# Sliding-window attention and a multiplicative FFN on one core: loads issued in one run, fold transposes a step ahead of their products, o units on column halves of TensorE in batches 0 and 1, and a new order of work for batch 1

**Chip, cores, metric.** One core of a Trainium2 chip. The metric is device time in microseconds (us) from launch to end. The "span" of a profile is 1.5 to 2 us shorter: first to last instruction.

## The reference, cut to what matters

```python
def _attn_ref(q, k, v):                    # (8, 8, 576, 64) each
    scores = (1 / sqrt(64)) * q @ k^T      # masked to 0 <= row - col < 64
    return softmax(scores) @ v

def _moe_ref(x, w1, w2, w3, w_out):        # x: (4608, 512), the attention's output
    return ((x @ w1) * (x @ w2)) @ w3 @ w_out      # d_ff = 1024
```

The kernel folds `w3 @ w_out` into one matrix `wc` once, runs attention batch by batch, and feeds nine groups of 512 tokens to the FFN. The part up to the end of token group 0 (batches 0 and 1, the fold, first FFN group) is written out by hand; I call it the prologue. After it comes a loop in which attention units lie between FFN steps.

Some names: a unit is one call of `scores` or `values` (four heads, 192 queries); units 0 to 5 are batch 0, 6 to 11 batch 1, and the first two of a batch have 768 columns, the others 1024. An FFN step is one call of `ffn_ab` or `ffn_o` (8 matmuls of 512 columns). A filler is a matmul of `keep_busy`, whose result nobody uses. A bank is the piece of PSUM that a matmul writes; the next writer waits until it is read (1.34 us at one unit of the run no_s). 1/sum is taken as Exp(-Ln(sum)).

## The kernel before: the parts that matter

```python
def load_rows(b, which):                         # q, k or v of a batch, cast to fp16 by the DMA
    t = sb.tile([P, 2, TI * D], FP16, name="rows")          # two buffers
    for hh in range(2):
        nc.gpsimd.dma_start(out=t[:, hh], in_=big_rows(which, b, hh))
    ...
def values(d, pool=None):                        # "o unit": probabilities x v, then 1/sum
    ...
    for jj in range(2):
        first = True
        for a in range(2):                       # v16 holds [v0 | ones | v1 | ones]
            c0 = 0
            for bi, (k0, q0, n, _) in enumerate(seg):
                o0 = a * 192 + q0 - q_base
                nc.tensor.matmul(o_ps[:, jj, o0:o0 + n],
                                 v16[:, si * 2 + bi, j0 + jj, a * D:a * D + P],   # 128 columns: o and sum
                                 pt[:, a, jj, c0:c0 + n],
                                 start=first, stop=(bi == 1), skip_group_check=True)
                first = False
                c0 += n
    ...
    nc.scalar.activation(y[0:D], o_ps[D:P, :, 0:192], AF.Ln)
    nc.scalar.activation(y[D:P], o_ps[0:D, :, 192:384], AF.Ln)
    nc.scalar.activation(r, y, AF.Exp, scale=-1.0)
    nc.vector.tensor_tensor(xs[0:D], o_ps[0:D, :, 0:192], r[0:D], ALU.mult)
    nc.vector.tensor_tensor(xs[D:P], o_ps[D:P, :, 192:384], r[D:P], ALU.mult)

def fold_t(fc, cp=dve_cp):      # 8 transposes of w3 into PSUM, copied back over w3
def fold_mm(fc, half, cp, nf=1):# 8 products of 256 columns (x nf), copied to wc

# fold stage (cut)
fold_t(0); scores(2); load_rows(1, "k"); fold_mm(0, 0, dve_cp)
fold_t(1); scores(3); fold_mm(1, 0, dve_cp)
fold_t(2); scores(4); fold_mm(2, 0, act_cp)
...
for d in range(3, 6):
    fold_mm(2 * d - 6, 1, dve_cp, 2)
    values(d, ps_s if d % 2 else None)
fold_mm(6, 1, dve_cp, 2)
for hh in range(2):
    cast_qk(1, "k", hh, dve_cp)
load_rows(1, "v")
for i in range(2):
    load_w12(i, 1)               # second halves of w1 and w2
# batch 1 (cut)
ffn_ab(0, 0)
transposes(1, "k", 0, 1, 2, ...)
ffn_ab(0, 1)
for hh in range(2):
    cast_qk(1, "q", hh, dve_cp)
transposes(1, "q", 0, 1, 2, ...)
ffn_ab(0, 2); scores(6); cast v; transposes v; ffn_ab(0, 3); scores(7) ...
```

## Time and profile before

| | us |
|---|---|
| device time, median of 3 runs (later, with more runs: 310.1 to 311.4) | 310.06 |
| first fold transposes start | 16.2 |
| eighth first-half fold product ends | 42.2 |
| second FFN step ends | 56.2 |
| first o unit of batch 1 starts | 72.2 |
| second token group starts | 95.6 |

These are start times on TensorE in the timeline; an end is the last start plus its length by starts (for the second FFN step, its end in the profile). From the last row on TensorE is busy nearly without a break (20.00 of the 20 us from 120 to 140), so what matters is how soon it comes. The lines behind it stand in the prediction.

### The profile page before, as it was taken

The numbers are of one execution on the slowest core, as the hardware profiler recorded it, in microseconds if no ns is written. First come the engines' busy times: TensorE is split into PE (matmuls) and PEld (weight loads), VectorE is DVE, ScalarE is ACT, GpSimd is POOL, SyncE is SP. The second block draws the span as 40 slices with busy tenths as digits, with TensorE's granted clock in tenths as the row PEclk, the third lists the DMA queues.
The fourth block names the chain that finished last, engine by engine and source line by source line (L and its number), as shares of the span: only waits on it lengthen the run. The fifth ranks groups of instructions, "written<-read, shape, count | busy, mean of one in ns | idle before, by whom it ended". The sixth has DMA issues, their size and how long they took to land.

```text
span 308.2 us, 6193 instructions
## 1 busy us (share of the span) xinstructions
PE 282.2 (92%) x2386; PEld 165.9 (54%) x2386; DVE 193.1 (63%) x300; ACT 173.1 (56%) x286; POOL 176.1 (57%) x212
## 2 busy tenths in 40 slices
PE   7675889778898999999999999999999999999992
PEld 7564786435464555555555588655555544454441
DVE  1534568735488676678878776667876765555531
ACT  2545544147843764777667756558657766642310
POOL 9799100267971995669687946486867544320400
PEclk9999799879999999999999999999999999999999
DMA  6999900999416993829483954092049003003012
GB/s 242 224 210 203 205 4 4 174 336 219 26 70 203 317 83 81 291 85 73 146 305 28 121 193 186 34 170 15 3 84 133 1 5 135 0 2 138 1 38 106
DMA packets 43906, 37.69 MB, mean 122 GB/s; under 512 B 29488, under 2 KB 33584, under 8 KB 43872
## 3 DMA queue, kind: packets, MB, share of 16 engines
q0 software_dynamic: 34560, 11.14, 32.8%
q1 hardware_dynamic: 9312, 26.10, 23.5%
q8 instruction: 20, 0.33, 0.4%
q14 instruction: 14, 0.11, 0.1%
HBM read 38.80 MB, written 9.44 MB: 156 GB/s over the span
## 4 chain that ended last, share of the span: by engine, by line
PE 76%; DVE 9%; ACT 5%; DMA 4%; issue 2%; POOL 2%; POOLq 0%; ACTq 0%; DVEq 0%
PE f_ps L413 36%; PE f_ps L426 20%; PE o_ps L329 5%; PE tp L261 5%; PE s_ps L295 4%; PE f_ps L477 3%; DMA ab<-in_moe_w_dram 3%; POOL v L512 2%; DVE xT L345 2%; DVE kT L265 2%; DMA stage<-in_k_dram 1%; ACT ln_s L339 1%; ACT r L341 1%; DVE xT L344 1%; ACT pt L299 1%
## 5 line engine op out<-in xcount | busy, mean ns | idle before, releaser
L413 PE MATMUL f_ps<-xT,w_sb 128*128 128x512 f16 (+1 forms) x640 | 137.1, 363 | 0.6 <-DVE xT L345 0.6
L307 POOL TENSOR_SCALAR_AFFINE_SELECT pt<-pt 128x512 f16<-128x512 f16 (+1 forms) x64 | 52.3, 818 | 70.6 <-ACT pt L299 70.6
L413 PEld LDWEIGHTS <-w_sb 128*128 128x128 f16 x640 | 60.6, 99 | 53.0 <-issue 4.5
L426 PE MATMUL f_ps<-wc_sb,ab 128*128 128x512 f16 x288 | 66.9, 379 | 0.1
L419 DVE TENSOR_TENSOR ab<-f_ps,a_sb 128x512 f16<-128x512 f32 x72 | 49.8, 692 | 21.2 <-PE f_ps L413 18.3
L299 ACT ACTIVATE pt<-s_ps 128x1024 f16<-128x1024 f32 (+1 forms) x48 | 45.6, 951 | 23.7 <-PE s_ps L295 22.2
L418 ACT COPY a_sb<-f_ps 128x512 f32<-128x512 f32 x72 | 41.7, 579 | 29.3 <-PE f_ps L413 28.7
L309 POOL TENSOR_SCALAR_AFFINE_SELECT pt<-pt 128x512 f16<-128x512 f16 (+1 forms) x64 | 51.9, 811 | 4.4
L344 DVE TENSOR_TENSOR xT<-o_ps,r 64x384 f16<-64x384 f32 x43 | 23.6, 550 | 47.3 <-ACT r L341 47.3
L426 PEld LDWEIGHTS <-ab 128*128 128x128 f16 x288 | 26.8, 98 | 28.2 <-issue 0.3
L338 ACT ACTIVATE ln_s<-o_ps 64x384 f32<-64x384 f32 x43 | 20.9, 487 | 36.8 <-PE o_ps L329 36.1
L428 DVE COPY t2k<-f_ps 128x512 f32<-128x512 f32 x36 | 24.8, 690 | 11.1 <-PE f_ps L426 10.6
L329 PEld LDWEIGHTS <-v 128*128 128x128 f16 x384 | 24.0, 99 | 12.2 <-ACT pt L299 3.9
L329 PE MATMUL o_ps<-pt,v 128*128 128x128 f16 x344 | 24.9, 216 | 1.7 <-DVE xT L345 1.7
L341 ACT ACTIVATE r<-ln_s 128x384 f32<-128x384 f32 x48 | 25.1, 522 | 1.5
L240 POOL DMA_DIRECT2D v<-in_v_dram x30 | 25.4, 854 | 0.0
L345 DVE TENSOR_TENSOR xT<-o_ps,r 64x384 f16<-64x384 f32 x43 | 24.1, 561 | 0.6
L339 ACT ACTIVATE ln_s<-o_ps 64x384 f32<-64x384 f32 x43 | 20.7, 482 | 0.5
L295 PEld LDWEIGHTS <-kT 64*128 64x128 f16 x384 | 10.6, 94 | 16.6 <-issue 15.0
L295 PE MATMUL s_ps<-qT,kT 64*128 64x128 f16 (+1 forms) x384 | 18.2, 214 | 0.5 <-ACT pt L299 0.4
L265 DVE COPY kT<-tp 128x768 f16<-128x768 f16 x17 | 16.2, 951 | 0.0
L225 POOL CAST k<-stage 128x1152 f16<-128x1152 f32 x12 | 13.8, 1151 | 2.0 <-PE tp L261 2.0
(83 smaller groups left out, 230.9 us busy)
## 6 DMA issues: line engine op xcount, KB each, us to landing
out_dram<-t2k SPq DMA_DIRECT2D x36, 256.0 KB
stage<-in_k_dram SPq DMA_DIRECT2D x14, 576.0 KB
stage<-in_q_dram SPq DMA_DIRECT2D x14, 576.0 KB
v<-in_v_dram POOLq DMA_DIRECT2D x24, 128.0 KB, 4.1
w_sb<-in_moe_w_dram POOLq DMA_DIRECT2D x4, 512.0 KB, 13.3
rows<-in_v_dram POOLq DMA_DIRECT2D x4, 288.0 KB, 8.0
ab<-in_moe_w_out_dram POOLq DMA_DIRECT2D x2, 512.0 KB, 11.9
ab<-in_moe_w_dram POOLq DMA_DIRECT2D x2, 512.0 KB, 9.3
```

The source lines that it names most:

```text
L295: nc.tensor.matmul(s_ps[:, a, jj, c0:c0 + n], kT[half, j, k0:k0 + P], qT[half, j, q0:q0 + n], start=True, stop=True, skip_group_check=True)
L299: nc.scalar.activation(pt[:, :, :, 0:w], s_ps[:, :, :, 0:w], AF.Exp, bias=-SHIFT, scale=scale)
L307: nc.gpsimd.affine_select(out=sl, in_=sl, pattern=pat, compare_op=ALU.is_ge, fill=0.0, base=off, channel_multiplier=-1)
L309: nc.gpsimd.affine_select(out=sl, in_=sl, pattern=[[-s, m] for s, m in pat], compare_op=ALU.is_ge, fill=0.0, base=63 - off, channel_multip ...
L329: nc.tensor.matmul(o_ps[:, jj, o0:o0 + n], v16[:, si * 2 + bi, j0 + jj, a * D:a * D + P], pt[:, a, jj, c0:c0 + n], start=first, stop=(bi = ...
L341: nc.scalar.activation(r, y, AF.Exp, scale=-1.0)
L344: nc.vector.tensor_tensor(xs[0:D], o_ps[0:D, :, 0:192], r[0:D], ALU.mult)
L345: nc.vector.tensor_tensor(xs[D:P], o_ps[D:P, :, 192:384], r[D:P], ALU.mult)
L413: nc.tensor.matmul(d[:, f * n + c0:f * n + c1], w[:, dc, (fc + f) * P:(fc + f + 1) * P], xT[:, dc, xc:xc + c1 - c0], start=first, stop=(dc ...
L418: act_cp(a_sb[:, 0:nf * n], a_ps[:, 0:nf * n])
L419: nc.vector.tensor_tensor(ab[:, fc:fc + nf, lo:hi], b_ps[:, 0:nf * n].rearrange("p (f n) -> p f n", f=nf), a_sb[:, 0:nf * n].rearrange("p ...
L426: nc.tensor.matmul(o_ps, ab[:, fc, t * P:t * P + P], wc_sb[:, fc, :], start=(fc == 0), stop=(fc == 7))
```

## The change

Its intent: issue the loads of batch 1 and the second halves of w1 and w2 early and in one run (three row buffers; three output buffers in place of four make room); turn each w3 block a step ahead of its product; shorten the chain after an o unit (Ln, Exp, multiply, up to the FFN's input xT); deal out the work of batch 1 so that TensorE has FFN steps to do while others cast and copy.

```diff
-        t = sb.tile([P, 2, TI * D], FP16, name="rows")
+        t = sb.tile([P, 2, TI * D], FP16, name="rows", bufs=3)
@@ values: for b < SHORT (= 2)
+            for jj in range(2):
+                c0 = 0
+                for bi, (k0, q0, n, _) in enumerate(seg):
+                    o0 = jj * 192 + q0 - q_base
+                    for e in range(2):            # e = 0: o, e = 1: sum
+                        for a in range(2):        # head a goes to column half a
+                            nc.tensor.matmul(o_ps[a * D:a * D + D, e, o0:o0 + n],
+                                             v16[:, si * 2 + bi, j0 + jj, (2 * a + e) * D:(2 * a + e) * D + D],
+                                             pt[:, a, jj, c0:c0 + n], ...)
+                    c0 += n
+            nc.scalar.activation(y, total, AF.Ln)
+            nc.scalar.activation(r, y, AF.Exp, scale=-1.0)
+            nc.vector.tensor_tensor(xs, o, r, ALU.mult)
+            return
@@ fold stage
     scores(2)
-    load_rows(1, "k")
+    fold_t(1, act_cp)
     fold_mm(0, 0, dve_cp)
-    fold_t(1)
     scores(3)
-    fold_mm(1, 0, dve_cp)
+    load_rows(1, "k")
     fold_t(2)
+    fold_mm(1, 0, act_cp)
 ...
     scores(5)
+    load_rows(1, "q")
+    for i in range(2):
+        load_w12(i, 1)
+    load_rows(1, "v")
+    fold_mm(3, 0, act_cp)
+    keep_busy(12)
 ...
-    for d in range(3, 6):
-        fold_mm(2 * d - 6, 1, dve_cp, 2)
+    for d in range(2, 6):
         values(d, ps_s if d % 2 else None)
-    fold_mm(6, 1, dve_cp, 2)
-    for hh in range(2):
-        cast_qk(1, "k", hh, dve_cp)
-    load_rows(1, "v")
-    for i in range(2):
-        load_w12(i, 1)
+        fold_mm(2 * d - 4, 1, dve_cp, 2)
+        if d == 4:
+            for hh in range(2):
+                cast_qk(1, "k", hh, dve_cp)
@@ batch 1: k transposes ahead of the first FFN step; q cast between steps 0 and 1; steps 4 and 5
@@ move ahead of the o units; the k transposes of batch 2 move in between them
```

More of the change, by code (lines that the diff above doesn't have):

```diff
@@ L169 @@
     ND = 6 * B
+    SHORT = 2
     keep = ctx.enter_context(tc.tile_pool(name="keep", bufs=1))
@@ L322, in values @@
             ps_s.tile([P, 2, 512], FP32, name="s_ps")
+        if jp == 0:
+            lns[b, si] = sb.tile([P, NJ, 192], FP32, name="ln_s", bufs=4)
+        y = lns[b, si][:, j0:j0 + 2]
+        r = sb.tile([P, 2, 192], FP32, name="r")
+        x0 = (b * S + q_base) % RING
+        xs = xT[:, j0:j0 + 2, x0:x0 + 192]
+        if b < SHORT:
+            for jj in range(2):
[6 more added lines that the diff above has]
+                                             v16[:, si * 2 + bi, j0 + jj, (2 * a + e) * D:(2 * a + e) * D + D],
+                                             pt[:, a, jj, c0:c0 + n],
+                                             start=(jj == 0 and bi == 0), stop=(bi == 1), skip_group_check=True)
+                    c0 += n
+            o, total = (o_ps[:, e, 0:384].rearrange("p (j n) -> p j n", j=2) for e in range(2))
+            nc.scalar.activation(y, total, AF.Ln)
+            nc.scalar.activation(r, y, AF.Exp, scale=-1.0)
+            nc.vector.tensor_tensor(xs, o, r, ALU.mult)
+            return
         for jj in range(2):
@@ L334, in values @@
                     c0 += n
-        if jp == 0:
-            lns[b, si] = sb.tile([P, NJ, 192], FP32, name="ln_s", bufs=4)
-        y = lns[b, si][:, j0:j0 + 2]
         nc.scalar.activation(y[0:D], o_ps[D:P, :, 0:192], AF.Ln)
         nc.scalar.activation(y[D:P], o_ps[0:D, :, 192:384], AF.Ln)
-        r = sb.tile([P, 2, 192], FP32, name="r")
         nc.scalar.activation(r, y, AF.Exp, scale=-1.0)
-        x0 = (b * S + q_base) % RING
-        xs = xT[:, j0:j0 + 2, x0:x0 + 192]
         nc.vector.tensor_tensor(xs[0:D], o_ps[0:D, :, 0:192], r[0:D], ALU.mult)
@@ L426, in ffn_o @@
             nc.tensor.matmul(o_ps, ab[:, fc, t * P:t * P + P], wc_sb[:, fc, :], start=(fc == 0), stop=(fc == 7))
-        o_sb = sb.tile([P, DM], FP32, name="t2k", bufs=4)
+        o_sb = sb.tile([P, DM], FP32, name="t2k", bufs=3)
         dve_cp(o_sb, o_ps)
@@ L549 @@
     scores(2)
+    fold_t(1, act_cp)
+    fold_mm(0, 0, dve_cp)
+    scores(3)
     load_rows(1, "k")
-    fold_mm(0, 0, dve_cp)
-    fold_t(1)
-    scores(3)
-    fold_mm(1, 0, dve_cp)
     fold_t(2)
+    fold_mm(1, 0, act_cp)
     scores(4)
+    fold_t(3)
     fold_mm(2, 0, act_cp)
-    fold_t(3)
     scores(5)
-    fold_mm(3, 0, dve_cp)
+    load_rows(1, "q")
[4 more added lines that the diff above has]
+    keep_busy(12)
     cast_qk(0, "v", 0, dve_cp)
-    cast_qk(0, "v", 1, act_cp)
-    load_rows(1, "q")
+    cast_qk(0, "v", 1, dve_cp)
     transposes(0, "v", 0, 1, 2, into=spare(ps_v, "o_ps") + [tp_bank()], cps=[dve_cp, act_cp, dve_cp])
     fold_t(4, act_cp)
-    fold_mm(4, 0, dve_cp)
-    keys_of_v(0, [0, 1, 2, 3], spare(ps_v, "o_ps") + spare(ps_s, "s_ps"), [dve_cp, act_cp, dve_cp, act_cp])
     fold_t(5)
+    keys_of_v(0, [0, 1], spare(ps_v, "o_ps"), [act_cp, dve_cp])
+    fold_mm(4, 0, act_cp)
+    keys_of_v(0, [2, 3], spare(ps_s, "s_ps"), [act_cp, dve_cp])
+    fold_t(6)
+    fold_mm(5, 0, dve_cp)
+    fold_t(7, act_cp)
     values(0)
-    fold_mm(5, 0, dve_cp)
-    fold_t(6)
+    fold_mm(6, 0, dve_cp)
     values(1, ps_s)
-    fold_mm(6, 0, dve_cp)
-    fold_t(7)
-    values(2)
     fold_mm(7, 0, dve_cp)
-    for d in range(3, 6):
-        fold_mm(2 * d - 6, 1, dve_cp, 2)
+    for d in range(2, 6):
         values(d, ps_s if d % 2 else None)
-    fold_mm(6, 1, dve_cp, 2)
-    for hh in range(2):
-        cast_qk(1, "k", hh, dve_cp)
-    load_rows(1, "v")
-    for i in range(2):
-        load_w12(i, 1)
+        fold_mm(2 * d - 4, 1, dve_cp, 2)
+        if d == 4:
+            for hh in range(2):
+                cast_qk(1, "k", hh, dve_cp)
     for n in range(3):
         keep_sums(n)
+    transposes(1, "k", 0, 1, 2, into=spare(ps_s, "s_ps") + [tp_bank()])
     ffn_ab(0, 0)
-    transposes(1, "k", 0, 1, 2, into=spare(ps_s, "s_ps") + [tp_bank()])
-    ffn_ab(0, 1)
     for hh in range(2):
         cast_qk(1, "q", hh, dve_cp)
-    load_qk(2, "k", nc.gpsimd.memset)
-    load_qk(2, "q")
+    ffn_ab(0, 1)
     transposes(1, "q", 0, 1, 2, into=spare(ps_v, "o_ps") + [tp_bank()])
@@ L600 @@
     cast_qk(1, "v", 0, dve_cp)
-    cast_qk(1, "v", 1, act_cp)
-    load_v(2, 0, 2, 3)
-    transposes(1, "v", 0, 1, 2, into=spare(ps_v, "o_ps") + [tp_bank()], cps=[dve_cp, act_cp, dve_cp])
+    cast_qk(1, "v", 1, dve_cp)
     ffn_ab(0, 3)
     scores(7)
+    load_qk(2, "k", nc.gpsimd.memset)
+    load_qk(2, "q")
+    transposes(1, "v", 0, 1, 2, into=spare(ps_v, "o_ps") + [tp_bank()], cps=[dve_cp, act_cp, dve_cp])
+    ffn_ab(0, 4)
+    scores(8)
+    load_v(2, 0, 2, 3)
     keys_of_v(1, [0, 1, 2], spare(ps_v, "o_ps") + [tp_bank()], [dve_cp, act_cp, dve_cp])
-    scores(8)
-    keys_of_v(1, [3], [tp_bank()], [dve_cp])
-    steps = [lambda fc=fc: ffn_ab(0, fc) for fc in range(4, 8)] + [lambda t=t: ffn_o(0, t) for t in range(4)]
+    ffn_ab(0, 5)
+    keys_of_v(1, [3], [tp_bank()], [act_cp])
+    steps = [lambda fc=fc: ffn_ab(0, fc) for fc in range(6, 8)] + [lambda t=t: ffn_o(0, t) for t in range(4)]
     for d in range(6, 12):
@@ L620 @@
             cast_qk(2, "kq"[(d - 6) // 2], d % 2, pool_cp)
-    transposes(2, "k", 0, 1, into=spare(ps_v, "o_ps"))
+        if d == 9:
+            transposes(2, "k", 0)
+        if d == 10:
+            transposes(2, "k", 1)
     transposes(2, "k", 2)
@@ L624 @@
         cast_qk(3, "k", hh, pool_cp)
-    steps.pop(0)()
-    store()
-    transposes(2, "q", 0, 1, into=spare(ps_s, "s_ps"))
-    transposes(2, "q", 2)
+    transposes(2, "q", 0, 1, 2, into=spare(ps_v, "o_ps") + spare(ps_s, "s_ps")[0:1])
     load_qk(3, "q")
-    steps.pop(0)()
-    store()
     copy_v(2, 1)
```

## The prediction

> **What bounds the kernel now.** I read the page's busy line first, then the same engines in stretches of 20 us, then the table of waits, then the timeline of the first 110 us. The page shows TensorE as the busiest engine, with 8% of the span free:
>
> ```profile
> span 308.2 us, 6193 instructions
> PE 282.2 (92%) x2386; PEld 165.9 (54%) x2386; DVE 193.1 (63%) x300; ACT 173.1 (56%) x286; POOL 176.1 (57%) x212
> ```
>
> The stretches (time, then busy us of PE, weight loads, DVE, ACT, POOL, then granted clock, DMA share, GB/s) show where the free part lies:
>
> ```profile
> 0.00:20.00 20.00, 14.83 (x218) 13.03 (x219) 7.26 (x10) 8.47 (x10) 16.68 (x26) 1.00 0.97 227
> 20.00:40.00 20.00, 13.78 (x164) 12.00 (x163) 10.08 (x17) 10.23 (x15) 11.70 (x13) 0.91 1.11 192
> 40.00:60.00 20.00, 16.87 (x166) 13.09 (x165) 15.15 (x26) 7.14 (x14) 2.67 (x5) 0.97 0.28 45
> 60.00:80.00 20.00, 15.84 (x142) 8.64 (x142) 9.65 (x16) 12.95 (x20) 13.21 (x18) 0.86 1.09 240
> 80.00:100.00 20.00, 18.66 (x152) 10.14 (x150) 15.33 (x25) 10.60 (x19) 11.58 (x12) 1.00 0.41 109
> 120.00:140.00 20.00, 20.00 (x171) 10.55 (x170) 14.46 (x23) 13.87 (x24) 12.48 (x17) 1.00 0.46 160
> ```
>
> From 100 us on TensorE has no idle time worth naming at full clock: whatever starts that part sooner ends the kernel sooner by as much. All idle time and both dips of the clock (0.91, 0.86) lie in the prologue: folding w3 with w_out, attention of batches 0 and 1, the first 512 tokens of the FFN. The first FFN product of the second token group starts at 95.6 us; 212 us follow. The change touches only that prologue. The table of waits and the timeline name its gaps:
>
> ```profile
> POOL rows L216 <- DVE k L225: 21.6, 1, 21.6
> DVE xT L344 <- ACT r L341: 50.4, 47, 1.7
> PE f_ps L477 <- DVE xT L469: 2.3, 3, 1.8
> PE f_ps L477 <- ACT xT L469: 2.0, 1, 2.0
> ```
>
> ```profile
> 17.59 1.05 PE L477 MATMUL f_ps<-ab 128*128 128x256 f16 x8 [0.46 <-DVE ab L469]
> 53.53 1.07 POOL L216 DMA_DIRECT2D rows<-in_v_dram  x2 [21.55 <-DVE k L225]
> 58.26 0.93 PE L261 MATMUL o_ps<-ident,q 128*128 128x128 f16 x12 [2.05 <-DVE q L225]
> 59.61 3.22 PE L413 MATMUL f_ps<-xT,w_sb 128*128 128x512 f16 x8
> 65.12 0.95 PE L261 MATMUL o_ps<-ident,k 128*128 128x128 f16 x12 [2.01 <-ACT k L225]
> ```
>
> The v load of batch 1 waited 21.6 us for one of two row buffers, and the second halves of w1 and w2 are queued behind it; the DMA was nearly idle meanwhile (45 GB/s in 40 to 60). Each fold product waits for the copy of its own transposes (0.46 to 2.0 us). TensorE then waits twice for 2 us on casts of q and v, after which an 8-matmul block takes 3.2 us in place of 1.9.
>
> [...] after gaps of 2 us with little work around them the same block ran at 3.22 against 1.90 us. [...] The trace has no column tiles; its row halves do pair up: eight 128-column score matmuls take 0.23 us of weight-load time where eight full ones take 0.45. [...]
>
> ```profile
> L338 ACT ACTIVATE ln_s<-o_ps 64x384 f32<-64x384 f32 x43 | 20.9, 487 | 36.8 <-PE o_ps L329 36.1
> L341 ACT ACTIVATE r<-ln_s 128x384 f32<-128x384 f32 x48 | 25.1, 522 | 1.5
> L344 DVE TENSOR_TENSOR xT<-o_ps,r 64x384 f16<-64x384 f32 x43 | 23.6, 550 | 47.3 <-ACT r L341 47.3
> ```
>
> **The change part by part.** I count TensorE work by starts: 0.46 us for a fold transpose, 0.87 for a fold product of one half (1.74 for two), 1.73 for an FFN step, 1.0 for 18 transposes, 0.3 for scores; copies by their rows: fold copy 0.69 on DVE or 1.02 on ACT, a transpose copy 0.95, a cast pair 0.83.
>
> *Short o units, 12 of them.* ACT loses one Ln (0.49), DVE one multiply (0.56): the chain from o to xT falls from 2 x 0.49 + 0.52 + 2 x 0.56 = 2.6 to 1.6 us. TensorE gets 16 half-width pairs for 8 full ones. If halves overlap it stays at 0.45 us; [...] I take 0.85, as the author keeps the old form where TensorE is the bound: +0.4 x 12 = 4.8 us of TensorE work.
>
> *Stage A, first fold transpose (16.2, set by a DMA) to the end of the eighth first-half fold product.* Before: ends at 42.2, with the three units 0 to 2. After: transposes run one step ahead, so a product waits for a copy that is mostly done. Stepping through, with the single score bank freed by ACT's exp (1.02) and ACT now also copying: fold 3 ends at 23.2 (25.3 before), 12 fillers to 23.9, v transposes at 23.9 (26.7), vT copied at 26.7, keys-of-v copies end 30.8, unit 0 at 31.1, unit 1 and products 6 and 7 end at 34.5. Unit 2 is not yet in: gain 7.7.
>
> *Stage B, to the end of the second FFN step.* Four units and four double products at 0.85 + 1.74, 1.0 of k transposes, two steps of 1.73: 34.5 + 10.4 + 1.0 + 3.5 = 49.4, against 56.2. Cumulative gain 6.8.
>
> *Stage C, to the first o unit of batch 1.* Before: 56.2 to 72.2, of which some 5 us are waits on casts, copies and small bank waits and 3 us the half clock; only two FFN steps inside. After: the rows came by about 47 us (1.6 MB more behind a queue that ends at 38.5 us, at the 205 GB/s of that part), casts lie beside FFN steps, four steps fill in: q transposes, 4 x 1.73, three scores, v transposes, 24 key transposes, small waits = 11.9, so 61.3. Two more steps (3.5) are already done: 16.0 + 3.5 - 11.9 = 7.6 gained. Cumulative 14.4.
>
> *Stage D, to the second token group.* Before: 72.2 to 95.6 = 23.4, less those two steps 19.9. After: six units, three scores, two FFN steps and four o steps, 36 transposes: 18.6 us, with POOL as a near tie. POOL has masks of six score units (2 x 2.1 + 4 x 2.25), v loads (4.3) and k casts (2.3) in a row: 54.1 + 20.5 = 74.6 before the last unit may start; TensorE by my count reaches it at 75.9. Gain 1.3; the second group starts at 79.9, 15.7 earlier.
>
> *Other edits.* Three buffers for output rows in place of four: copies are at least 1.7 us apart even at the tail, so I give this nothing. DMA, total bytes: unchanged.
>
> From 15.7 I take off 2.6 for handovers and shared-bank waits that such stepping misses (of the kind that show as 0.2 to 0.6 us all over the timeline). 310.1 - 13.1 = **297.0 us**.
>
> **The rivals.**
> (1) *POOL becomes the bound of stages C and D.* Its work from the first scores of batch 1 on is 20 us that nothing shortens, and batch 2's loads now start only after the second masks, so its first cast might wait. For it: POOL runs from 73 to 88 us without a break now. Against: k of batch 2 has some 9 us to land. If it holds, stage D loses 3 to 5 us: 300 to 302.
> (2) *Column halves are dear.* If halves do not overlap at all[...]: 12 x 0.3 to 0.5 more, 300 to 303.
> (3) *Full gain.* Halves overlap (0.45 a unit) and nothing is missed: 4 to 5 us better than my sum before the deduction, 291 to 292.
> (4) *The idle time is only moved.* The second group begins early, but q of batch 2 or the cast of batch 3 is late, and TensorE waits at 80 to 95 us. Now only about 2 us are lost there; I see no reason for over 3 more.
>
> **Range and chances.** Rivals 1 and 2 together make about 303, rival 3 makes 291: range 291 to 303. Faster by 2% needs under 303.9, that is, 6.2 of the counted 15.7 us: 0.89. Within 2%: 0.09. Slower: 0.02; nothing is added to the TensorE-bound part.
>
> **What would show it.** The second group's first FFN product at 79 to 85 us, and the same 212 us after it; clock near 1.00 from 20 us on and DMA busy to about 47 us without the pause; no POOL wait for a row buffer; fold products waiting under 0.4 us; one Ln and one multiply of 128x384 at about 0.50 and 0.57 us a unit; 16 half-width matmuls in about 0.85 us. I am wrong if the second group starts after 89 us, if a unit holds TensorE over 1.2 us, if the part after it grows by over 3 us, or if POOL or a late load becomes the longest wait in 50 to 80 us.

## The result

293.60 us median (four runs, 292.96 to 295.06) against 310.59 (four runs, 309.82 to 311.32). The ratio is 0.946, 95% interval 0.9413 to 0.9507. Ratios here are the mean time of one kernel's fast runs over that of the other's of the same rounds, so not quite the ratio of the medians quoted. Taken as 5.4% of 310.6, the gain is 16.8 us; I had predicted 13.1.

The page and the stretches of the changed kernel (same columns as before):

```profile
span 293.3 us, 6375 instructions
PE 281.0 (96%) x2494; PEld 165.4 (56%) x2494; DVE 185.3 (63%) x284; ACT 168.4 (57%) x278; POOL 176.5 (60%) x212
```

```profile
20.00:40.00 20.00, 18.94 (x275) 15.86 (x274) 11.65 (x18) 13.18 (x21) 15.66 (x20) 1.00 1.20 207
40.00:60.00 20.00, 19.59 (x208) 12.68 (x206) 16.01 (x25) 8.85 (x15) 4.42 (x9) 1.00 0.40 70
60.00:80.00 20.00, 19.15 (x217) 10.64 (x215) 11.05 (x18) 11.93 (x21) 17.75 (x18) 1.00 1.38 248
80.00:100.00 20.00, 19.31 (x168) 10.17 (x166) 15.68 (x24) 13.34 (x23) 17.52 (x22) 1.00 0.89 215
```

TensorE's busy time has hardly changed (282.2 to 281.0 us), its idle time has. From 20 to 80 us it was busy for 46.5 us in the kernel before (13.78 + 16.87 + 15.84) and for 57.7 us now, at full clock. The timeline of the changed kernel, line by line against that of before:

```profile
19.12 1.05 PE L496 MATMUL f_ps<-ab 128*128 128x256 f16 x8
...
34.01 0.50 ACT L344 ACTIVATE ln_s<-o_ps 128x384 f32<-128x384 f32 x1
34.54 0.52 ACT L345 ACTIVATE r<-ln_s 128x384 f32<-128x384 f32 x1
35.09 0.56 DVE L346 TENSOR_TENSOR xT<-o_ps,r 128x384 f16<-128x384 f32 x1 [1.44 <-ACT r L345]
...
50.47 0.84 PE L262 MATMUL o_ps<-ident,q 128*128 128x128 f16 x12 [0.33 <-DVE q L226]
...
51.48 1.89 PE L432 MATMUL f_ps<-xT,w_sb 128*128 128x512 f16 x8
...
73.50 0.51 PE L262 MATMUL tp<-ident,k 128*128 128x128 f16 x6 [0.85 <-POOL k L226]
...
80.32 1.89 PE L432 MATMUL f_ps<-xT,w_sb 128*128 128x512 f16 x8
```

The first fold product (19.12) shows no wait for its copy. One Ln, one Exp and one multiply on 128x384 replace five instructions (0.50, 0.52, 0.56 us). The q transposes wait 0.33 us for their cast in place of 2.05, and the FFN block after them runs in 1.89 us in place of 3.22 (in the kernel before the granted clock was 0.50 from 60 to 62 us, within that block; now it is 1.00 from 40 to 60 us). One wait remains that I had named as a danger: 0.85 us for GpSimd's cast of k at 73.5. The second token group starts at 80.3.

| | before | counted in the prediction | after |
|---|---|---|---|
| first fold transposes start | 16.2 | 16.2 | 17.7 |
| eighth first-half product ends | 42.2 | 34.5 | 35.8 |
| second FFN step ends | 56.2 | 49.4 | 50.1 |
| first o unit of batch 1 | 72.2 | 61.3 | 62.2 |
| second token group | 95.6 | 79.9 | 80.3 |
| from there to the end of the span | 212.6 | 212.6 | 213.0 |

In this run the fold began 1.5 us late, in a first stretch at clock 0.91 (15 fillers took 1.49 us in place of 1.00); it is the slowest of the four runs (295.06), and the other three left no trace. Seen from the first fold transposes the second group comes after 62.6 us, against 63.7 counted.

### The profile page after: what moved, and what is told of

The parts are those of the page before. It is cut to its first block, busy times and chain, and to the rows that moved or that the text cites.

```text
span 293.3 us, 6375 instructions
## 1 busy us (share of the span) xinstructions
PE 281.0 (96%) x2494; PEld 165.4 (56%) x2494; DVE 185.3 (63%) x284; ACT 168.4 (57%) x278; POOL 176.5 (60%) x212
## 4 chain that ended last, share of the span: by engine, by line
PE 84%; DVE 6%; POOL 4%; issue 2%; ACT 1%; POOLq 0%; ACTq 0%
PE f_ps L432 37%; PE f_ps L445 20%; PE o_ps L354 5%; PE tp L262 5%; PE s_ps L296 5%; PE f_ps L496 4%; PE tp L522 4%; POOL v L241 1%; DVE kT L266 1%; DVE k L226 1%; POOL pt L308 1%; PE o_ps L262 1%; PE f_ps L487 1%; DVE qT L266 1%; POOL k L226 1%
## 5 line engine op out<-in xcount | busy, mean ns | idle before, releaser
L432 PE MATMUL f_ps<-xT,w_sb 128*128 128x512 f16 (+1 forms) x640 | 134.2, 358 | 0.0
L432 PEld LDWEIGHTS <-w_sb 128*128 128x128 f16 x640 | 59.7, 98 | 50.3 <-issue 0.3
L438 DVE TENSOR_TENSOR ab<-f_ps,a_sb 128x512 f16<-128x512 f32 x72 | 49.8, 691 | 19.2 <-PE f_ps L432 14.4
L363 DVE TENSOR_TENSOR xT<-o_ps,r 64x384 f16<-64x384 f32 x36 | 19.8, 550 | 39.7 <-ACT r L362 39.7
L360 ACT ACTIVATE ln_s<-o_ps 64x384 f32<-64x384 f32 x36 | 17.5, 487 | 32.6 <-PE o_ps L354 32.6
L354 PEld LDWEIGHTS <-v 128*128 128x128 f16 x288 | 18.1, 98 | 8.7 <-ACT pt L300 0.8
L354 PE MATMUL o_ps<-pt,v 128*128 128x128 f16 (+1 forms) x288 | 20.7, 215 | 0.4 <-DVE xT L364 0.4
L364 DVE TENSOR_TENSOR xT<-o_ps,r 64x384 f16<-64x384 f32 x36 | 20.2, 561 | 0.5
L362 ACT ACTIVATE r<-ln_s 128x384 f32<-128x384 f32 x36 | 18.8, 522 | 1.1
L266 DVE COPY kT<-tp 128x768 f16<-128x768 f16 x19 | 18.1, 951 | 0.7 <-PE tp L262 0.7
L361 ACT ACTIVATE ln_s<-o_ps 64x384 f32<-64x384 f32 x36 | 17.4, 482 | 0.4
```

What stands on the lines that cost most here:

```text
L266: cp(dst.rearrange("q j (p i) -> q j p i", i=TI)[:, :, :, 6 * c:6 * c + 6], tp.rearrange("q i (p j) -> q j p i", p=TP))
L354: nc.tensor.matmul(o_ps[:, jj, o0:o0 + n], v16[:, si * 2 + bi, j0 + jj, a * D:a * D + P], pt[:, a, jj, c0:c0 + n], start=first, stop=(bi = ...
L432: nc.tensor.matmul(d[:, f * n + c0:f * n + c1], w[:, dc, (fc + f) * P:(fc + f + 1) * P], xT[:, dc, xc:xc + c1 - c0], start=first, stop=(dc ...
L438: nc.vector.tensor_tensor(ab[:, fc:fc + nf, lo:hi], b_ps[:, 0:nf * n].rearrange("p (f n) -> p f n", f=nf), a_sb[:, 0:nf * n].rearrange("p ...
```

## The experiments

All twelve gave correct results. Of the kernel before, three of the runs beside them were slow (one in group 1, two beside ones_dve); the ratios leave them out. The kernels of a group ran on one chip together with the kernel before (ones_dve later, on another chip). The changed kernel itself was not run again beside them, so I compare ratios to the kernel before; by their intervals a difference of two ratios is known to some 2 us either way.

### Group 1: one part alone, on the kernel before

**l_only**, the early loads alone:

```diff
-        t = sb.tile([P, 2, TI * D], FP16, name="rows")
+        t = sb.tile([P, 2, TI * D], FP16, name="rows", bufs=3)
-        ... name="t2k", bufs=4)
+        ... name="t2k", bufs=3)
     load_rows(1, "q")
+    for i in range(2):
+        load_w12(i, 1)
+    load_rows(1, "v")          # and not after the fold stage
```

> The kernel before with the loads of the change alone (three row buffers, v rows of batch 1 and the second halves of w1 and w2 issued right after the q rows; output buffers three as the space asks). Theory 1 (order of TensorE work is what pays, the early loads only make room for it): no wait of TensorE in the kernel before ends with a load between 40 and 80 us, so within 1 us of before, about 310, though the DMA pause at 38 to 54 us goes. Theory 2 (the late loads cost the time): 5 us or more faster, 305 or less.

Measured: 311.94 us against 311.24, ratio 1.0045 (0.9991 to 1.0099). The pause of the DMA shrank, as its stretch shows (DMA share and GB/s are the last two columns; it was 0.28 and 45):

```profile
40.00:60.00 20.00, 17.64 (x154) 13.61 (x154) 14.98 (x26) 7.43 (x15) 0.00 (x0) 0.91 0.63 155
```

By its ratio it is 1.4 us slower, within noise. The longest single wait named in the prediction (21.6 us) thus cost nothing that these runs can resolve: TensorE did not wait for what was queued behind it.

**s_only**, the short o units of batches 0 and 1 alone (the branch `if b < SHORT` put into the kernel before):

> The kernel before with the short o units in batches 0 and 1 alone. Theory 1: a unit costs TensorE about 0.1 us more, and the chain from o to xT is 1 us shorter; this shows only where that chain paces TensorE (units 6 to 8, which now follow each other by 3.4 us, to about 2.7): 1.5 to 3 us faster, about 308. Theory 2 (a shorter chain pays in all 12 units): 6 us or more faster. Theory 3 (column halves are dear, 0.85 us a unit as I had predicted): 0 to 1 us.

Measured: 306.04 us, ratio 0.989 (0.9835 to 0.9945): 3.4 us faster, a little above theory 1. Units 6 to 8 follow each other by 2.8 us (69.7, 72.8, 75.4) where they took 3.6 before (72.2, 76.0, 79.3), and the fold stage gains some from shorter waits for DVE. In these two profiles some 1.2 us of the fold stage are clock and not the edit: from 31.3 us on the kernel before took 3.12 us for the 24 key transposes and fold transposes that s_only did in 1.94 (granted clock 0.54 from 31.3 to 34.5 us in the kernel before, 1.00 from 20 to 40 us in s_only). The clock varies from run to run (a mean of 0.967 to 0.991 in the eleven runs of the kernel before), so the mean of six runs counts, not this pair.

**f_only**, the order of the fold stage alone (the fold stage of the diff with the loads left in their old places):

> The kernel before with the order of the fold stage of the change alone (transposes one step ahead, products and copies dealt out anew), full o units, old loads, old order from batch 1 on. Theory 1: it saves the waits of products for their own copies, most of stage A: 5 to 7 us, about 304. Theory 2 (the time only moves to the casts and loads of batch 1): under 2 us.

Measured: 303.26 us, ratio 0.9777 (0.9716 to 0.9839): 6.9 us faster, the top of theory 1. The largest part by itself. Not all of it need be the waits: the fold stage's order brings 12 fillers, and the stretch from 20 to 40 us ran at clock 1.00, where the kernel before had 0.91 and l_only, with the old order, 0.83. No run tests the fillers alone.

**bl_only**, the early loads and the new order from batch 1 on, with the old fold stage and full units:

```diff
+    (loads as in l_only)
-    ffn_ab(0, 0)
-    transposes(1, "k", 0, 1, 2, ...)
-    ffn_ab(0, 1)
+    transposes(1, "k", 0, 1, 2, ...)
+    ffn_ab(0, 0)
+    (cast q) ; ffn_ab(0, 1) ; ... as in the change, to the end of the prologue
```

> The kernel before with the early loads and the order of the change from batch 1 on (two more FFN steps ahead of the o units, transposes of batch 2 among them), old fold stage, full o units. Theory 1: waits on casts and the half clock go, stages C and D save 9 us less the 2 that the short units bring there: 6 to 8 us, about 303. Theory 2 (without the short units the ACT chain takes it back): 3 us or less.

Measured: 307.63 us, ratio 0.9911 (0.985 to 0.9973): 2.8 us faster, well below theory 1. The timeline shows where the rest went:

```profile
56.32 0.84 PE L261 MATMUL s_ps<-ident,k 128*128 128x128 f16 x12 [2.62 <-DVE k L225]
...
76.60 0.50 PE L329 MATMUL o_ps<-pt,v 128*128 128x128 f16 x8 [1.18 <-DVE xT L345]
```

The k transposes now come first after the fold stage, and in the old fold stage the cast of k is the last thing that DVE does, behind the copies on DVE: a new wait of 2.6 us. And the full units pace TensorE: units 7, 8 and 9 wait 1.18, 0.71 and 0.38 us. So theory 2's number came, for two reasons of which it had named one.

### Group 2: the changed kernel less one part, and the short unit itself

**no_s**, full units everywhere:

```diff
-    SHORT = 2
+    SHORT = 0
```

> The changed kernel with full o units everywhere. Theory 1: twelve units give back 0.1 us of TensorE time each, but the longer chain paces units 0 to 11 now that little else does: 3 to 6 us slower than the changed kernel, 297 to 300. Theory 2 (short units are a detail): within 1 us of it.

Measured: 297.68 us, ratio to the kernel before 0.9595 (0.9566 to 0.9624), against 0.946 for the changed kernel: about 4.2 us are the short units' (0.0135 x 310). The waits that come back:

```profile
36.27 0.61 PE L354 MATMUL o_ps<-pt,v 128*128 128x128 f16 x8 [1.34 <-DVE xT L364]
...
46.66 0.84 PE L262 MATMUL s_ps<-ident,k 128*128 128x128 f16 x12 [1.46 <-DVE xT L364]
...
67.07 0.50 PE L354 MATMUL o_ps<-pt,v 128*128 128x128 f16 x8 [1.18 <-DVE xT L364]
...
70.44 0.61 PE L354 MATMUL o_ps<-pt,v 128*128 128x128 f16 x8 [0.71 <-DVE xT L364]
```

All four are waits for the PSUM bank of an earlier unit, until its second multiply is done. Together 4.7 us.

**no_l**, the loads late again:

```diff
-        ... name="rows", bufs=3)
+        ... name="rows")
-    for i in range(2):
-        load_w12(i, 1)
-    load_rows(1, "v")          # moved back behind the fold stage
```

> The changed kernel with two row buffers and the v rows of batch 1 and the second halves of w1 and w2 issued after the fold stage, as before. They would be issued at some 45 to 48 us and land at 53 to 58; v is cast at 54.5 and the second half of w1 first read at 56.8. Theory 1 (early loads make room for the new order and no more): 1 to 3 us slower, 294.5 to 297. Theory 2 (early loads are the core): over 5 us slower.

Measured: 294.00 us, ratio 0.9473 (0.944 to 0.9506). That is the changed kernel's time within noise, less than even theory 1 had expected. In its profile the q transposes wait 0.33 us for their cast and the FFN steps run on, as in the changed kernel. It was close: the DMA falls quiet at about 55.5 us, the v transposes start at 55.3 and the first step that reads the second halves at 56.3. With l_only the two groups agree: the early loads, first in the change's own description, gave no measurable part of the gain.

**s_all**, short units in all eight batches:

```diff
-    SHORT = 2
+    SHORT = 8
```

> The changed kernel with short o units in all eight batches. Theory 1: each unit holds TensorE about 0.1 us longer (0.57 against 0.45 from the start of a full-width unit to the start of what follows), and from 83 us on TensorE is the bound: 36 units x 0.12 = 4 us slower, about 297.5, while ACT and DVE lose 17 and 20 us of work. Theory 2 (column halves pair without cost): within 1 us.

Measured: 301.52 us, ratio 0.9711 (0.9681 to 0.9741): by the ratios 7.8 us slower than the changed kernel, twice what theory 1 had said. In the TensorE-bound part, first the changed kernel, where this unit is a full one (FFN step, unit, next step):

```profile
124.68 1.89 PE L432 MATMUL f_ps<-xT,w_sb 128*128 128x512 f16 x8
126.41 0.61 PE L354 MATMUL o_ps<-pt,v 128*128 128x128 f16 x8
126.86 1.89 PE L445 MATMUL f_ps<-wc_sb,ab 128*128 128x512 f16 x8
```

and the same unit in s_all:

```profile
124.95 1.89 PE L432 MATMUL f_ps<-xT,w_sb 128*128 128x512 f16 x8
126.77 0.64 PE L338 MATMUL o_ps<-pt,v 128*64 128x128 f16 x16
127.34 1.90 PE L445 MATMUL f_ps<-wc_sb,ab 128*128 128x512 f16 x8
```

By starts, the full unit takes 0.45 us and the short one 0.57. That is the 0.12 I had seen. But the FFN step ahead of it also holds TensorE longer, 1.82 us in place of 1.73. So a short unit costs 0.12 + 0.09 = 0.21 us more, and 36 of them 7.6, near the measured 7.8. The trace shows the 0.09 on entry, as before the score matmuls, which use row halves (their FFN step takes 1.82 or 1.83 too). The trace does not name its cause. The cost explains why the change keeps short units out of the loop.

**no_pair**, the same 16 matmuls of a short unit, first all of one column half, then all of the other:

```diff
-            for jj in range(2):
-                for bi, ... in enumerate(seg):
-                    for e in range(2):
-                        for a in range(2):
+            for a in range(2):
+                for jj in range(2):
+                    for bi, ... in enumerate(seg):
+                        for e in range(2):
```

> The changed kernel with the matmuls of a short unit in another order: all of one column half, then all of the other, so that neighbours share a half (same matmuls, same results). Theory 1 (the halves work side by side): a unit of 1024 columns holds TensorE for about 0.9 us in place of 0.57, 12 units: 3 to 4 us slower at most. Theory 2 (they do not, and a half-width matmul is merely short): no change.

Measured: 295.87 us, ratio 0.9534 (0.9497 to 0.9571): 2.3 us slower than the changed kernel. A 1024-column unit, changed kernel and then no_pair:

```profile
35.89 0.64 PE L338 MATMUL o_ps<-pt,v 128*64 128x128 f16 x16
36.46 1.92 PE L496 MATMUL f_ps<-ab 128*128 128x256 f16 x16
```

```profile
35.48 0.89 PE L338 MATMUL o_ps<-pt,v 128*64 128x128 f16 x16
36.30 1.92 PE L496 MATMUL f_ps<-ab 128*128 128x256 f16 x16
```

0.57 us with the halves in turn, 0.82 one after the other. In turn that is 36 ns a matmul, which fits halves that work side by side; in the other order 16 matmuls take 51 ns each, no sign of overlap (8 full ones take 0.45 us, 56 ns each). Twelve units at about 0.2 to 0.25 us give 2.4 to 3.0, near the 2.3 measured (known to 2 us either way).

### Group 3: the new order of batch 1, and an attempt to go further

**no_b**, the changed kernel with the old order from batch 1 on:

> The changed kernel with the order of the kernel before from batch 1 on (short units, early loads and new fold stage kept). Alone, on the old fold stage, the new order brought only 3 us, of which a 2.6 us wait of TensorE for the k cast took part. Theory 1 (it needs the k cast that the new fold stage puts inside its products; then it saves the casts' waits and the half clock): 6 to 8 us slower than the changed kernel, about 300.5. Theory 2 (it is worth the same 3 us here): about 297.

Measured: 299.95 us, ratio 0.9647 (0.9598 to 0.9695): 1.9% or 5.8 us over the changed kernel. That is just under theory 1's range and twice the 2.8 us of bl_only. The 2 us waits for the casts of q and v and the slow FFN blocks after them (3.43 and 3.40 us in place of 1.89) are all back in its timeline:

```profile
50.67 0.84 PE L262 MATMUL o_ps<-ident,q 128*128 128x128 f16 x12 [2.06 <-DVE q L226]
...
51.82 3.43 PE L432 MATMUL f_ps<-xT,w_sb 128*128 128x512 f16 x8
...
57.53 0.84 PE L262 MATMUL o_ps<-ident,k 128*128 128x128 f16 x12 [2.01 <-ACT k L226]
...
58.72 3.40 PE L432 MATMUL f_ps<-xT,w_sb 128*128 128x512 f16 x8
```

**ones_late**, GpSimd's weight loads ahead of its two fills of ones:

```diff
-    ones_of(0)
-    ones_of(1)
     load_wo(0)
     ...
     load_wo(1)
+    ones_of(0)
+    ones_of(1)
```

> An attempt to go further: the changed kernel with GpSimd's two fills of ones (5.25 us) put behind its weight loads, so that these are issued from 1.5 us on in place of 6.6. Theory 1 (the fold stage starts when its first w3 rows land, and the next loads follow): they come 2 to 4 us sooner, but TensorE's program puts fillers and scores first, so 0 to 1.5 us faster. Theory 2 (the loads now take bandwidth from k and q of batch 0, which come first): 1 to 3 us slower.

Measured: 299.98 us, ratio 0.9658 (0.9616 to 0.97): some 6 us slower than the changed kernel, outside both theories. Its timeline:

```profile
6.62 7.08 DVE L229 CAST k<-stage 128x768 f16<-128x768 f32 x2 [6.62 <-DMA stage<-in_k_dram]
7.47 5.34 POOL L531 MEMSET v<- 128x3072 f16 x2
```

k landed when it always did (6.6 us), so theory 2 is not the cause. But DVE's two casts of k, 1.5 us long in the changed kernel, took 7.1 us around GpSimd's fill. The run shows that the fill holds the cast: the pair is on record from 6.62 to 13.70 us, the fill from 7.47 to 12.81, and TensorE's first transposes of k, which wait for the cast, start at 13.29, after the fill. By what means the one holds the other, the trace does not show. In the kernels before and after, the fill ends at 6.65 us, just as k lands.

**tuned**, ones_late, with the first fold work in place of the fillers between the first scores, and one k cast of batch 2 on DVE:

```diff
     scores(0)
-    keep_busy(12)
-    scores(1)
     (load_w12)
-    keep_busy(12)
     fold_t(0)
+    scores(1)
+    fold_t(1)
+    fold_mm(0, 0, dve_cp)
     scores(2)
 ...
-            cast_qk(2, "kq"[(d - 6) // 2], d % 2, pool_cp)
+            cast_qk(2, "kq"[(d - 6) // 2], d % 2, dve_cp if d == 7 else pool_cp)
```

> As the attempt with late fills, and besides the first fold transposes and products take the place of the fillers between the first scores (one score unit earlier throughout), and one of GpSimd's casts of k of batch 2 goes to DVE, as TensorE waits 0.85 us for it. Theory 1: 1.5 to 2 us from the fold stage and about 1 us from the cast: 290.5 to 291.5. Theory 2 (the w3 rows come too late to fill those places, or k and q come later): no faster than the changed kernel.

Measured: 297.84 us, ratio 0.9584 (0.9543 to 0.9624): 2.1 us faster than ones_late and still some 4 us slower than the changed kernel, as the two casts of k take 7.0 us here too. TensorE no longer waits for the k cast of batch 2.

**ones_dve**, as tuned, but DVE does the two fills at the start, while it is idle:

```diff
-        nc.gpsimd.memset(v16s[i]..., 1.0)
+        nc.vector.memset(v16s[i]..., 1.0)
```

> The last attempt with late fills (fold work in place of fillers, one k cast on DVE), but with the two fills of ones done by DVE at the very start, where it has nothing to do until k lands at 6.6 us; GpSimd then issues its loads from 1.5 us on and is quiet while k is cast. Theory 1 (GpSimd's fill held DVE's cast of k for 5 us in the two attempts before: the pair of casts took 7.0 us around a fill of 5.3): the pair of casts is back at 1.5 to 2 us, the second group starts 5 us sooner than in the last attempt, 290.5 to 292.5 in all. Theory 2 (the early weight loads took the bandwidth of k and q): k and q stay late, 296 or more.

Measured: 293.44 us against 310.31, ratio 0.9468 (0.9426 to 0.9509). That GpSimd's fill held the casts is confirmed: with the same early loads and GpSimd not filling, the pair of casts is back at 1.05 us, though it starts 0.7 us later, behind DVE's own fills.

```profile
7.35 1.05 DVE L229 CAST k<-stage 128x768 f16<-128x768 f32 x2
...
15.67 0.62 PE L487 MATMUL f_ps<-ident,ab 128*128 128x128 f16 x8 [0.27 <-DMA ab<-in_moe_w_dram]
```

But it does not beat the changed kernel. The first w3 rows were issued 5 us sooner and the fold still waits for them until 15.7 us, where the kernel before waited until 16.2; q now lands at 11.6 us (10.1 before). That part of theory 2 is true: the DMA moved hardly more in the first 20 us than in the kernel before (231 and 227 GB/s), so it seems that the earlier issue only reordered the bytes. I found no version that is clearly faster than the changed kernel.

### What each part is worth

| part | alone, on the kernel before | missing from the changed kernel |
|---|---|---|
| early loads | -1.4 (slower, in noise) | 0.4 (in noise) |
| short units | 3.4 | 4.2 |
| fold order | 6.9 | not run |
| order of batch 1 (with loads) | 2.8 | 5.8 |

Times are in us, each from its ratio, each known to some 2 us. Alone, the parts that count add up to 13.1 us of the 16.8. The difference is little more than the noise of such a sum, but the traces show where it lies: without the early k cast of the fold order and the short chain of the units, the order of batch 1 meets waits of 2.62 us and of 1.18, 0.71 and 0.38 us (bl_only), which the changed kernel does not have.

## Why the prediction was right, and where it was off

**The bound and the method** held. The part after the second token group takes the same time in both kernels (212.6 and 213.0 us), so the gain is how much sooner it starts. As lengths, the four stages took 18.1, 14.4, 12.0 and 18.1 us, where 18.3, 14.9, 11.9 and 18.6 had been counted. That rows and casts came in time, that waits of about 2 us and the half clock went (the granted clock from 60 to 80 us was 0.86 and is 1.00), and that the chain fell to one Ln and one multiply: the traces show all three.

**The size was off by 3.7 us**, from two terms of the sum. One is the TensorE time of a short unit, put at 0.85 us, an estimate of mine that no trace had shown. It is 0.57 us, or 0.47 for the units of 768 columns, and 0.09 more on entry, 0.63 on average: 12 x 0.22 = 2.7 us too much. The other is the deduction of 2.6 us "for handovers and shared-bank waits that such stepping misses". Such waits came to some 1.6 us (0.78 for the vT copies at 28.8, 0.85 for GpSimd at 73.5), so 1.0 us too much. This is a balance of one profile counted from its first fold transposes, not a test of each term. The two margins were partly one caution taken twice: with the deduction left out the count says 294.4, against 293.6 measured.

**Slips in its working** that did not move the number: GpSimd's list for stage D adds up to 19.8 us, not 20.5; the waits of fold products for their copies are 0.2 to 2.0 us, not 0.46 to 2.0; and rival 3's 4 to 5 us below the undeducted sum would be 289 to 290, not 291 to 292, so the lower end of the range was drawn too high for its own argument.

**The loads** were over-read. I showed the 21.6 us wait of GpSimd and the DMA pause among the named gaps, and let stage C rest on rows that "came by about 47 us". l_only and no_l show that neither the pause nor the early issue matters. The number did not suffer, as the sum had no term for the loads, but the reader was pointed at the wrong line. The sign was there: no wait of TensorE in the table ended with a load between 40 and 80 us.

**The rivals.** GpSimd as the bound of stage D was real but small: 0.85 us of the 3 to 5 I had allowed. Dear column halves: no, a unit took 0.57 us. "Full gain" was nearest in kind, as the halves in turn take 0.57 us against 0.82 one after the other, but a unit is not back at 0.45 us and some waits came. Moved idle time: no, TensorE lost 0.7 us from 80 to 100 us, where I had allowed 3.

## What to carry to other kernels

Before crediting a wait, ask what the waiting thing feeds: a wait of 21.6 us on GpSimd was free, while waits of 0.5 to 2.6 us of TensorE, the engine that sets the end, and the slow FFN blocks after them (3.22 us in place of 1.89) were where the gain lay. Where several engines hand a product on, put the producer one step ahead and give the bounding engine independent work in the gap; test such reorderings together, as one may need the slot that another opens (here the k cast that the fold order moves forward). A form that shortens the chain but costs the bounding engine time belongs only in the part where the chain paces: 4 us gained in 12 units of the prologue, 8 us lost in 36 units of the loop.

## What these runs measured of the hardware

- The step ahead of a unit on column halves (s_all, 124.95 us) or of row-half scores (the changed kernel, 113.11 us) takes 1.82 us in place of 1.73 (the changed kernel, 124.68 us), that is 0.09 us for each entry.
- 16 half-width matmuls of 128 columns take 0.57 us when neighbours use different halves (the changed kernel, 35.89 us) and 0.82 us when they do not (no_pair, 35.48 us).
- The weight loads of these units, 16 of 64 columns, span 0.48 us (30 ns each) with the halves in turn (the changed kernel, 35.89 us) and 0.73 us one half after the other (no_pair, 35.47 us). Whether each load is slow and they overlap, or is fast, these runs don't tell.
- Before each slow FFN block (3.2 to 3.4 us in place of 1.9) lie 3.2 to 3.4 us with nothing on TensorE but a wait of 2.0 us and 18 transposes (1.2 to 1.4 us), in the five kernels that share that order (before, l_only, s_only, f_only, no_b). What in that stretch makes the block slow, these runs don't tell. Elsewhere the clock is a matter of the run: the mean clock of the kernel before lay between 0.967 and 0.991 in the eleven runs of group 1.
